# v_m summed in PSUM by one split-factor matmul per token and batch, and a softmax on VectorE and ScalarE alone

## The chip, the core and the metric

The kernel runs on one core of a Trainium2 chip. The metric is device time in microseconds, the median of several executions.

## What is computed

Attention over 32 memory slots per head, followed by a mixture-of-depths layer. Eight batches, 8 heads, 576 tokens, head dimension 64; the layer picks 128 tokens of each batch.

```python
a = phi - np.max(phi, axis=2, keepdims=True)          # over the tokens
a = np.exp(a)
a = a / (np.sum(a, axis=2, keepdims=True) + 1e-09)
k_m = np.einsum('bhsm,bhsd->bhmd', a, k)
v_m = np.einsum('bhsm,bhsd->bhmd', a, v)
scores = scale * np.matmul(q, k_m.transpose(0, 1, 3, 2))
attn = softmax(scores)                                # over the slots
x = np.matmul(attn, v_m)                              # then heads side by side: (B, S, 512)
# layer, per batch b:
scores[b] = x[b] @ w_gate
top_idx = np.argpartition(-scores[b], 128)[:128]
ye = np.maximum(x[b, top_idx] @ w1, 0.0) @ w2
out[b, top_idx] = x[b, top_idx] + sigmoid(scores[b, top_idx])[:, None] * ye
```

The choice of tokens hangs on the last bits of the scores, so the first softmax and v_m are computed in float32 with the reference's roundings.

## The kernel before

A group is four heads (two pairs) of a batch: 128 partitions of (head, slot) by 576 tokens. There are 16 groups, two to a batch.

`softmax(b, g)` (L161) computes a for a group. exp is a rational function whose multiply-adds are rounded once: `step_fma` (L192) splits both factors and carries the error, with ScalarE making the high halves, GpSimd nearly all products and differences (L198 to L209), VectorE one correction (L206). The quotient uses a reciprocal (L227) and more GpSimd work. At the end ScalarE and GpSimd make `half0` and `half1` (L261, L262), the high and low parts of a.

`keys(b, g)` (L268) transposes a to tokens on partitions (`aS`) and makes k_m, which goes into the block diagonal `kbd`.

`values(b, r, beside)` (L291) makes v_m of a pair of heads. For each of the 32 slots TensorE spreads the slot's row of a over 64 partitions for each head, by two float32r matmuls with the constant `sel` (L300), and VectorE multiplies that with v and sums over the tokens in one instruction (L303). After each slot `beside(m)` takes a step of the jobs that run between the sums: the next group's keys and softmax, and the attention and layer of the batch before.

`attention_and_ffn(b)` (L522) is `centre` (v_m less its mean, into `vbd`), three times `scores` and `attend`, then `rank`, `gather`, `ffn1`, `ffn2`. In `attend` GpSimd adds the means (L419); `score` (L386) makes the gate scores on VectorE (L389 to L394).

The order of instructions on each engine is the order of the program. Loads are issued on SyncE's queue; the stores of x and the indirect DMAs on GpSimd's. The weights w1 and w2 are loaded near the start by `late_consts`.

Of the kernel before, what the change touches and what calls it, by code (L numbers as in the profile page):

```python
# [13 lines left out]
I32 = mybir.dt.int32  # L14
AF = mybir.ActivationFunctionType
# [13 lines left out]
ROUND = 1.5 * 2.0 ** 23  # L29
# [4 lines left out]
EXP_LOWEST = -87.0  # L34


@with_exitstack
def kernel(
    ctx: ExitStack,
    tc: tile.TileContext,  # L40
    qT: bass.AP,      # [B, steps, (2h d), pairs, (2c p)], token p * NC + c
    k: bass.AP,       # [B, groups, p, c, (4h d)], token c * PT + p
    vT: bass.AP,      # [B, pairs, (2h d), s]
    phiT: bass.AP,    # [B, groups, (4h m), s]
# [3 lines left out]
    out: bass.AP,     # [B, S, D]  # L48
# [5 lines left out]
    PT = S // NC            # partitions of tokens  # L54
    NJ = qT.shape[1]        # steps of two columns of tokens
    NPR = vT.shape[1]       # pairs of heads
    NG = phiT.shape[1]      # groups of four heads, that is of two pairs
# [5 lines left out]
    HS = S // 2  # L63
# [3 lines left out]
    # The chosen tokens, in rows of at most 128 ranks.  # L67
# [5 lines left out]
    io = ctx.enter_context(tc.tile_pool(name="io", bufs=2))  # L73
    ex = ctx.enter_context(tc.tile_pool(name="ex", bufs=1))
    work = ctx.enter_context(tc.tile_pool(name="work", bufs=2))
    one = ctx.enter_context(tc.tile_pool(name="one", bufs=1))
    step = ctx.enter_context(tc.tile_pool(name="step", bufs=2))
    psb = ctx.enter_context(tc.tile_pool(name="psb", bufs=3, space=PSUM))
    pss = ctx.enter_context(tc.tile_pool(name="pss", bufs=2, space=PSUM))
# [4 lines left out]
    phis, ks, vs, qs = {}, {}, {}, {}  # L84

    def load_phi(b, g):
        phis[b, g] = io.tile([P, S], F32, name="ph")
        nc.sync.dma_start(out=phis[b, g], in_=phiT[b, g])

    def load_kv(b, g):  # L90
        ks[b, g] = io.tile([PT, NC, D // NG], F32, name="kb")
        nc.sync.dma_start(out=ks[b, g], in_=k[b, g])
        for r in (2 * g, 2 * g + 1):
            vs[b, r] = io.tile([P, S], F32, name="vb", bufs=4)
            nc.sync.dma_start(out=vs[b, r], in_=vT[b, r])

    def load_q(b, j):
        qs[b, j] = io.tile([P, NPR, 2 * PT], F32, name="qb", bufs=3)
        nc.sync.dma_start(out=qs[b, j], in_=qT[b, j])

    load_phi(0, 0)
    load_phi(0, 1)
    load_kv(0, 0)
    load_kv(0, 1)
# [5 lines left out]
    sel = const.tile([P, M, 2 * Dh], F32R, name="sel")  # L110
    nc.gpsimd.memset(sel.bitcast(F32), 0.0)
    for rr in range(2):
        for u in range(2):
            part = sel[:, :, u * Dh:(u + 1) * Dh]
            nc.gpsimd.affine_select(out=part, in_=part.bitcast(F32), compare_op=ALU.not_equal, fill=1.0,
                                    base=-(2 * rr + u) * M, pattern=[[-1, M], [0, Dh]],
                                    channel_multiplier=1)
    # k_m and v_m of several heads as block diagonals; what is off them stays zero.
    kbd = [const.tile([P, NPR, 2 * M], F32, name=f"kbd{i}") for i in range(2)]
    vbd = [const.tile([P, 2, NPR * Dh], F32, name=f"vbd{i}") for i in range(2)]  # L120
    for t in kbd + vbd:
        nc.vector.memset(t, 0.0)

    w1_sb = const.tile([P, KD, F], F32, name="w1_sb")
    w2_sb = const.tile([P, KF, D], F32, name="w2_sb")
# [5 lines left out]
    def late_consts():  # L131
# [3 lines left out]
        nc.sync.dma_start(out=w1_sb, in_=w1.rearrange("(t p) f -> p t f", p=P))  # L135
        nc.sync.dma_start(out=w2_sb, in_=w2.rearrange("(t p) f -> p t f", p=P))
# [4 lines left out]
        # wide[p, n] = 1 where n - (NC - 1) * PT < p.  # L141
# [9 lines left out]

    biases = {}
    for x in (EXP_P[0], EXP_P[1], EXP_P[2], EXP_P[4], EXP_Q[1], -1.0, -ROUND):
        biases[x] = constant(x)

    def fma(dst, src, s, c):
        nc.scalar.activation(dst, src, AF.Identity, bias=biases[c], scale=s)  # L157

    soft = {}

    def softmax(b, g):  # L161
        """a = exp(phi - max) / sum over the tokens, as numpy rounds it, and by pairs of heads
# [53 lines left out]
        for c in (EXP_P[2], EXP_P[1], EXP_P[0]):  # L216
            yield from step_fma(num, num, c)
# [387 lines left out]
```

## Time and profile before

| | |
|---|---|
| median of 3 runs | 1953.56 us (1953.15 to 1955.42) |
| span of the profiled execution | 1954.3 us |
| VectorE busy | 1352.5 us, 69% |
| GpSimd busy | 1041.0 us, 53% |
| TensorE busy | 996.6 us, 51% |
| ScalarE busy | 294.2 us, 15% |
| DMA | 52.0 MB, 27 GB/s on average |

The span runs from the first to the last instruction of one execution; the profiled execution's own time is known only by this span, which lies within the spread of the three runs. A busy share is a mean over stages whose limits differ. Matmuls are pipelined, so the busy time of TensorE counts overlapping records once and is not its throughput. [...]

### The profile page before, as it was taken

The numbers are of one execution on the slowest core, as the hardware profiler recorded it, in microseconds if no ns is written. First come the engines' busy times: TensorE is split into PE (matmuls) and PEld (weight loads), VectorE is DVE, ScalarE is ACT, GpSimd is POOL, SyncE is SP. The second block draws the span as 40 slices with busy tenths as digits, with TensorE's granted clock in tenths as the row PEclk, the third lists the DMA queues.
The fourth block names the chain that finished last, engine by engine and source line by source line (L and its number), as shares of the span: only waits on it lengthen the run. The fifth ranks groups of instructions, "written<-read, shape, count | busy, mean of one in ns | idle before, by whom it ended". The sixth has DMA issues, their size and how long they took to land. (4 is left out here: it accounts for less than half of the span.)

```text
span 1954.3 us, 13765 instructions
## 1 busy us (share of the span) xinstructions
PE 996.6 (51%) x4088; PEld 767.7 (39%) x4088; DVE 1352.5 (69%) x3052; ACT 294.2 (15%) x505; POOL 1041.0 (53%) x734
## 2 busy tenths in 40 slices
PE   0256363473635645366443655437463374634944
PEld 0244252352524434254432544325352352524733
DVE  2568677766876668757688567875687856877743
ACT  1111121111211112111120112101121111111010
POOL 8594837347473555627376092752927438373021
PEclk9955566575666657565665756657566575765666
DMA  4001011000000010010100101001010100100000
GB/s 152 12 7 37 11 33 30 24 24 30 27 17 24 24 32 26 16 36 12 43 22 8 42 6 43 22 9 42 6 43 22 32 24 18 44 18 6 6 16 19
DMA packets 17915, 52.00 MB, mean 27 GB/s; under 512 B 2096, under 2 KB 2096, under 8 KB 17840
## 3 DMA queue, kind: packets, MB, share of 16 engines
q1 hardware_dynamic: 13872, 37.49, 6.2%
q0 software_dynamic: 3968, 13.63, 2.3%
q8 instruction: 32, 0.52, 0.1%
q14 instruction: 43, 0.35, 0.1%
HBM read 39.58 MB, written 11.53 MB: 26 GB/s over the span
## 5 line engine op out<-in xcount | busy, mean ns | idle before, releaser
L300 PE MATMUL sp<-half,sel 128*128 128x288 f32 x2048 | 673.1, 473 | 706.5 <-DVE junk L303 546.7
L303 DVE SCALAR_TENSOR_TENSOR junk<-sp,vb 128x576 bf16<-128x576 f32 x1024 | 720.8, 748 | 233.5 <-PE sp L300 233.5
L300 PEld LDWEIGHTS sp<-half,sel 128*128 128x128 f32 x2048 | 469.8, 286 | 869.2 <-DVE junk L303 692.0
L389 DVE TENSOR_TENSOR prod<-xj,wg 96x1024 f32<-96x1024 f32 x24 | 113.7, 4736 | 101.8 <-POOL xj L419 101.8
L419 POOL TENSOR_TENSOR xj<-xj,mean 96x1024 f32<-96x1024 f32 x48 | 115.1, 2398 | 74.4 <-DVE xj L415 72.5
L190 POOL TENSOR_TENSOR rl<-r,rh 128x576 f32<-128x576 f32 x16 | 20.4, 1275 | 238.5 <-ACT rh L188 238.5
L208 POOL TENSOR_TENSOR low<-low,big 128x576 f32<-128x576 f32 x64 | 89.9, 1405 | 106.2 <-DVE big L206 102.9
L206 DVE SCALAR_TENSOR_TENSOR big<-s,big 128x576 f32<-128x576 f32 x64 | 67.9, 1061 | 110.3 <-ACT s L157 110.3
L262 POOL TENSOR_TENSOR half<-a,half 64x576 fp32r<-64x576 f32 x32 | 44.7, 1397 | 155.2 <-issue 141.6
L517 POOL DMA_INDIRECT out<-ye,idx x8 | 8.1, 1017 | 212.9 <-DVE ye L515 212.9
L204 POOL TENSOR_TENSOR low<-low,vl 128x576 f32<-128x576 f32 x64 | 109.3, 1708 | 5.0
L198 POOL TENSOR_TENSOR vl<-num,vh 128x576 f32<-128x576 f32 x48 | 61.2, 1276 | 86.5 <-ACT vh L197 86.5
L412 PE MATMUL bank<-vbd,eT 128*96 128x256 f32 x192 | 88.7, 616 | 31.4 <-ACT eT L406 31.4
L203 POOL TENSOR_TENSOR vl<-vl,r 128x576 f32<-128x576 f32 x64 | 104.4, 1632 | 0.0
L303 DVE DVE_READ_ACCUMULATOR junk<-sp,vb 128x1 f32 x1024 | 82.6, 81 | 0.0
L202 POOL TENSOR_TENSOR low<-vh,rl 128x576 f32<-128x576 f16 x64 | 82.4, 1287 | 0.2
L157 ACT ACTIVATE s<-big,c 128x576 f32<-128x576 f32 x64 | 49.5, 774 | 218.2 <-POOL big L199 218.2
L199 POOL TENSOR_TENSOR big<-vh,rh 128x576 f32<-128x576 f16 x64 | 81.3, 1271 | 0.0
L498 PE MATMUL bank<-xeT,w_sb 128*128 128x128 f32 x512 | 73.3, 313 | 13.7 <-ACT xeT L492 13.7
L498 PEld LDWEIGHTS bank<-xeT,w_sb 128*128 128x128 f32 x512 | 71.3, 227 | 15.8 <-ACT xeT L492 15.8
L209 POOL TENSOR_TENSOR num<-s,low 128x576 f32<-128x576 f32 x48 | 73.5, 1531 | 3.8
L434 PE MATMUL bank<-ident,gate 96*96 96x96 f32 x48 | 10.3, 307 | 123.2 <-DVE gate L394 113.4
(121 smaller groups left out, 1508.2 us busy)
## 6 DMA issues: line engine op xcount, KB each, us to landing
kb<-in_k SPq DMA_DIRECT2D x16, 576.0 KB, 4.5
vb<-in_vT SPq DMA_DIRECT2D x32, 288.0 KB, 2.8
qb<-in_qT SPq DMA_DIRECT2D x24, 384.0 KB, 4.4
out<-xj POOLq DMA_DIRECT2D x24, 384.0 KB, 3.3
ph<-in_phiT SPq DMA_DIRECT2D x16, 288.0 KB, 3.4
w_sb<-in_w SPq DMA_DIRECT2D x2, 2048.0 KB, 16.2
wg<-in_w_gate SPq DMA_DIRECT2D x1, 256.0 KB, 10.7
xe<-out,idx POOLq DMA_INDIRECT x8, 3.4
```

The lines of the kernel that those rows point to most:

```text
L199: nc.gpsimd.tensor_mul(big, vh, rh)
L202: nc.gpsimd.tensor_mul(low, vh, rl)
L203: nc.gpsimd.tensor_mul(vl, vl, r)
L204: nc.gpsimd.tensor_add(low, low, vl)
L208: nc.gpsimd.tensor_sub(low, low, big)
L209: nc.gpsimd.tensor_add(dst, s, low)
L300: nc.tensor.matmul(out=sp[:, hf, :HS], lhsT=sel[:, m], rhs=parts[:, hf * HS:(hf + 1) * HS], start=True, stop=True)
L303: nc.vector.scalar_tensor_tensor(out=junk, in0=sp[:, :, :HS], scalar=1.0, in1=vb.rearrange("p (a n) -> p a n", a=2), op0=ALU.mult, op1=ALU ...
L389: nc.vector.tensor_mul(prod[:n, :cols], rows, wg[:n].unsqueeze(1).to_broadcast([n, cols, D]))
L412: nc.tensor.matmul(out=o[:, u].rearrange("p r d -> p (r d)"), lhsT=eT[:, c, u], rhs=vbd[b % 2][:, u], start=True, stop=True)
L419: nc.gpsimd.tensor_add(x, x, t.unsqueeze(1).to_broadcast([PT, 2, D]))
L498: nc.tensor.matmul(out=ps[:, f, :n], lhsT=w1_sb[:, d, (f0 + f) * P:(f0 + f + 1) * P], rhs=xeT[:, d, :n], start=(d == 0), stop=(d == KD - 1))
```

## The change

- The reference's sum over tokens for v_m moves to TensorE. a and v are each split in a high and a low part (bits masked off, and the difference), so that a product of two parts is exact, and a matmul per token and batch, with the parts and heads on 32 rows, adds the four products of all 8 heads into a PSUM bank. The rows off the block diagonal of `a_rows` and half of `v_rows` stay zero.
- To have tokens in sequence and (head, part) on partitions, the parts go through DRAM: `split_v` writes `vparts` (each part twice), `keys` writes `aparts`, both from GpSimd's queue, and `values` reads them back in chunks of 36 tokens for four batches, from SyncE's queue, into two buffers.
- `sel`, the halves and VectorE's sums are gone. `centre` transposes v_m first.
- The softmax uses integer high parts on a grid (written as int16 by ScalarE), no GpSimd and no reciprocal of 576 columns.
- The order: `turns` interleaves two jobs, the second `lag` steps after the first; `beside` takes n steps of another job after each. Softmax of batches 0 to 3 with `split_v` of all batches; softmax of batches 4 to 7 with the sums of batches 0 to 3; attention of batches 0 to 3 with the sums of batches 4 to 7; attention of batches 4 to 7.
- GpSimd zeroes the tiles. w1 and w2 are loaded when the attention begins. `load_q` is issued by `scores`, a step ahead. `kbd` has a tile for each batch.

```diff
+    kbd = [const.tile([P, NPR, 2 * M], F32, name=f"kbd{i}") for i in range(B)]
+    v_rows = [rows.tile([P, 2, T, Dh], F32R, name=f"v_rows{i}") for i in range(2)]
+    a_rows = [rows.tile([P, T, NPR, M], F32R, name=f"a_rows{i}") for i in range(2)]
+    for t in v_rows + a_rows:
...
     def softmax(b, g):
+        r = phis.pop((b, g))
+        mx = ex.tile([P, 1], F32, name="mx")
+        nc.vector.tensor_reduce(mx, r, axis=AX.X, op=ALU.max)
+        nc.vector.tensor_scalar(out=r, in0=r, scalar1=mx, scalar2=EXP_LOWEST,
                                 op0=ALU.subtract, op1=ALU.max)
+        q = t("q", I16)
+        act(q, r, LOG2E)
+        yield
+        for ln2 in (LN2_HI, LN2_LO):
+            stt(out=r, in0=q, scalar=-ln2, in1=r, op0=ALU.mult, op1=ALU.add)
+        rh, rl = t("rh", I16), t("rl")
+        act(rh, r, 2.0 ** 11)
         num, den = t("num"), t("den")
+        act(num, r, EXP_P[5] * UP, EXP_P[4] * UP)
+        dh = t("dh", I16)
+        act(dh, r, EXP_Q[2] * UP * GRID, EXP_Q[1] * UP * GRID)
+        act(den, r, EXP_Q[2] * UP, EXP_Q[1] * UP)
+        yield
+        tt(out=num, in0=num, in1=r, op=ALU.mult)
+        vh = t("vh", I16)
+        act(vh, num, GRID, EXP_P[3] * UP * GRID)
+        act(num, num, 1.0, EXP_P[3] * UP)
+        stt(out=rl, in0=rh, scalar=-GRID, in1=r, op0=ALU.mult, op1=ALU.add)
+        def fma(val, h, c):
+            lo, big, low = t("lo"), t("big"), t("low")
+            stt(out=lo, in0=val, scalar=GRID, in1=h, op0=ALU.mult, op1=ALU.subtract)
+            tt(out=big, in0=h, in1=rh, op=ALU.mult)
+            tt(out=lo, in0=lo, in1=rh, op=ALU.mult)
+            tt(out=low, in0=val, in1=rl, op=ALU.mult)
+            tt(out=low, in0=low, in1=lo, op=ALU.add)
+            stt(out=val, in0=big, scalar=c * UP, in1=low, op0=ALU.add, op1=ALU.add)
+        yield
+        fma(den, dh, EXP_Q[0])
+        dh = t("dh", I16)
+        act(dh, den, GRID / 2)
+        y0 = t("y0", I16)
+        act(y0, r, 1.0, Y0_SCALE, AF.Exp)
         for c in (EXP_P[2], EXP_P[1], EXP_P[0]):
+            yield
+            fma(num, vh, c)
+            if c != EXP_P[0]:
+                vh = t("vh", I16)
+                act(vh, num, GRID)
+            if c == EXP_P[2]:
+                sq = t("rl2")
+                act(sq, den, 1.0 / UP, -1.5, AF.Square)
+        dl, p = t("lo"), t("big")
+        stt(out=dl, in0=den, scalar=GRID / 2, in1=dh, op0=ALU.mult, op1=ALU.subtract)
+        stt(out=p, in0=sq, scalar=0.75, in1=den, op0=ALU.add, op1=ALU.mult)
+        s2 = t("low")
+        act(s2, p, 1.0 / UP, -1.5, AF.Square)
+        tt(out=p, in0=y0, in1=dh, op=ALU.mult)
+        tt(out=num, in0=num, in1=p, op=ALU.subtract)
+        tt(out=dl, in0=y0, in1=dl, op=ALU.mult)
+        tt(out=num, in0=num, in1=dl, op=ALU.subtract)
+        two_q = t("den", I32)
+        yield
+        act(two_q, q, UP, 127 * UP)
+        stt(out=num, in0=s2, scalar=0.75, in1=num, op0=ALU.add, op1=ALU.mult)
+        stt(out=num, in0=sq, scalar=0.75, in1=num, op0=ALU.add, op1=ALU.mult)
+        stt(out=num, in0=num, scalar=GRID, in1=y0, op0=ALU.mult, op1=ALU.add)
+        sm = ex.tile([P, 4], F32, name="sm")
         e = t("e")
+        stt(out=e, in0=num, scalar=GRID / 2, in1=two_q.bitcast(F32),
+            op0=ALU.mult, op1=ALU.mult, accum_out=sm[:, 0:1])
...
         for i in (2, 3):
+            stt(out=e, in0=a0, scalar=sm[:, i:i + 1], in1=e, op0=ALU.mult, op1=ALU.add)
+        stt(out=e, in0=e, scalar=sm[:, 1:2], in1=a0, op0=ALU.mult, op1=ALU.add)
+        soft[b, g] = e
+        yield
+        yield from keys(b, g)
+    def split_v(b):
         for u in range(2):
+            vb = io.tile([P, S * Dh * NPR // P], F32, name="vb")
+            nc.sync.dma_start(out=vb, in_=v[b, u])
+            hi = io.tile([P, S * Dh * NPR // P], F32, name="vhi")
+            nc.vector.tensor_single_scalar(hi.bitcast(I32), vb.bitcast(I32), -4096,
+                                           op=ALU.bitwise_and)
+            nc.vector.tensor_sub(vb, vb, hi)
+            yield
+            for vp, src in enumerate((vb, hi)):
+                for ap in range(2):
+                    nc.gpsimd.dma_start(
+                        out=vparts[b, u, ap, vp].rearrange("r s d -> (r s d)")
+                                                .rearrange("(p x) -> p x", p=P), in_=src)
+            yield
...
     def keys(b, g):
...
+        hi = ex.tile([PT, NC, P], F32, name="ahi", bufs=1)
+        lo = ex.tile([PT, NC, P], F32, name="alo", bufs=1)
+        nc.vector.tensor_single_scalar(hi.bitcast(I32), aS.bitcast(I32), -4096,
+                                       op=ALU.bitwise_and)
+        nc.vector.tensor_sub(lo, aS, hi)
+        for h in range(4):
+            r, u = 2 * g + h // 2, h % 2
+            for part, src in enumerate((lo, hi)):
+                nc.gpsimd.dma_start(
+                    out=aparts[r, b, u, part].rearrange("(c p) m -> p c m", p=PT),
+                    in_=src[:, :, h * M:(h + 1) * M])
...
+    def values(st):
+        accs = [accp.tile([P, 512], F32, name=f"acc{i}") for i in range(SET)]
+        b0 = st * SET
+        def load(ch):
+            ss = slice(ch * T, (ch + 1) * T)
+            for vp in range(2):
+                for r in range(NPR):
+                    nc.sync.dma_start(
+                        out=a_rows[ch % 2][vp * 4 + r::8, :, r].bitcast(F32),
+                        in_=aparts[r, b0:b0 + SET].rearrange("b u t s m -> (b u t) s m")[:, ss])
+            for bb in range(SET):
+                for u in range(2):
+                    p0 = bb * 32 + u * 16
+                    nc.sync.dma_start(
+                        out=v_rows[ch % 2][p0:p0 + 16, u].rearrange("p s d -> p (s d)").bitcast(F32),
+                        in_=vparts[b0 + bb, u].rearrange("t w r s d -> (t w r) (s d)")
+                            [:, ch * T * Dh:(ch + 1) * T * Dh])
+        n = S // T
+        load(0)
+        for ch in range(n):
+            if ch + 1 < n:
+                load(ch + 1)
+            vr, ar = v_rows[ch % 2], a_rows[ch % 2]
+            for s in range(T):
+                for bb in range(SET):
+                    p = slice(bb * 32, bb * 32 + 32)
+                    nc.tensor.matmul(out=accs[bb][:, :P].rearrange("p (u d) -> p u d", d=Dh),
+                                     lhsT=ar[p, s].rearrange("p r m -> p (r m)"), rhs=vr[p, :, s],
+                                     start=(ch == 0 and s == 0), stop=(ch == n - 1 and s == T - 1))
+                if s % 4 == 3:
+                    yield
+        for bb in range(SET):
+            v_m[b0 + bb] = const.tile([P, P], F32, name=f"v_m{b0 + bb}")
+            nc.scalar.activation(v_m[b0 + bb], accs[bb][:, :P], AF.Copy)
...
+        tp = bank([P, P])
+        nc.tensor.transpose(out=tp, in_=v_m.pop(b), identity=ident)
+        vm = work.tile([P, NPR, M], F32, name="vmT")
+        nc.scalar.activation(vm.rearrange("p r m -> p (r m)"), tp, AF.Copy)
...
+    def turns(jobs, lag, width=2):
+        jobs, live, since = list(jobs), [], lag
+        while jobs or live:
+            if jobs and len(live) < width and since >= lag:
+                live.append(jobs.pop(0))
+                since = 0
+            since += 1
+            for job in list(live):
+                if next(job, live) is live:
+                    live.remove(job)
+                else:
+                    yield
+    def beside(main, other, n):
+        for _ in main:
+            for _ in range(n):
+                next(other, None)
+            yield
+    def group(i):
+        if i + 2 < len(groups):
+            load_phi(*groups[i + 2])
+        load_k(*groups[i])
+        yield from softmax(*groups[i])
...
+    half = len(groups) // 2
+    finish(beside(turns([group(i) for i in range(half)], 6),
+                  chain(*[split_v(b) for b in range(B)]), 1))
+    sums = values(0)
+    finish(beside(turns([group(i) for i in range(half, 2 * half)], 6), sums, 2))
+    finish(sums)
+    first.close()
+    w1_sb = one.tile([P, KD, F], F32, name="w1_sb")
+    w2_sb = one.tile([P, KF, D], F32, name="w2_sb")
+    nc.sync.dma_start(out=w1_sb, in_=w1.rearrange("(t p) f -> p t f", p=P))
+    nc.sync.dma_start(out=w2_sb, in_=w2.rearrange("(t p) f -> p t f", p=P))
+    def batch(b):
+        load_q(b, 0)
+        yield from attention_and_ffn(b)
+    sums = values(1)
+    finish(beside(turns([batch(b) for b in range(SET)], 10), sums, 2))
+    finish(sums)
+    finish(turns([batch(b) for b in range(SET, B)], 10))
...
```

`act(dst, src, s, c, func)` is a ScalarE activation of s * src + c; `tt` and `stt` are VectorE's tensor_tensor and scalar_tensor_tensor. SET is 4, T is 36.

## Rows read from the trace of the kernel before

**Rows 1.** The page: span, and its first part (busy share of each engine).

```profile
span 1954.3 us, 13765 instructions
...
PE 996.6 (51%) x4088; PEld 767.7 (39%) x4088; DVE 1352.5 (69%) x3052; ACT 294.2 (15%) x505; POOL 1041.0 (53%) x734
```

**Rows 2.** Window of one batch: stretch, length, PE, PEld, DVE, ACT, POOL busy, clock, DMA.

```profile
301.00:523.00 222.00, 119.41 (x500) 92.21 (x498) 159.12 (x365) 34.35 (x59) 119.54 (x84) 0.62 0.08 24
```

**Rows 3.** Waits in that batch: who waited for whom, us in total, times, longest.

```profile
DVE junk L303 <- PE sp L300: 31.9, 16, 7.3
...
ACT s L157 <- POOL big L199: 26.7, 7, 7.9
...
PE sp L300 <- POOL half L262: 10.2, 2, 5.2
...
DVE prod L389 <- POOL xj L419: 10.2, 2, 5.1
```

**Rows 4.** Groups by form: busy us, mean ns of one, idle before.

```profile
L303 DVE SCALAR_TENSOR_TENSOR junk<-sp,vb 128x576 bf16<-128x576 f32 x1024 | 720.8, 748 | 233.5 <-PE sp L300 233.5
...
L206 DVE SCALAR_TENSOR_TENSOR big<-s,big 128x576 f32<-128x576 f32 x64 | 67.9, 1061 | 110.3 <-ACT s L157 110.3
...
L227 DVE RECIPROCAL s<-den 128x576 f32<-128x576 f32 x16 | 59.8, 3740 | 0.0
...
L178 DVE SCALAR_TENSOR_TENSOR x<-q,x 128x576 f32<-128x576 f32 x16 | 12.0, 752 | 7.2 <-ACT q L157 7.2
...
L174 DVE TENSOR_SCALAR q<-x 128x576 f32<-128x576 f32 x16 | 9.2, 572 | 0.5
```

**Rows 5.** Window of the last batch's attention and layer.

```profile
1859.00:1954.30 95.30, 41.51 (x195) 31.77 (x195) 36.94 (x81) 9.96 (x21) 17.64 (x11) 0.64 0.06 18
```

**Rows 6.** Timeline at the start: start us, length us, engine, line.

```profile
1.34 3.50 POOL L111 MEMSET sel<- 128x4096 f32 x1
...
1.73 0.42 SPq L92 DMA_DIRECT2D kb<-in_k  x1
```

**Rows 7.** Windows of the weight loads (w1, then w2).

```profile
14.00:18.00 4.00, 0.00 (x0) 0.00 (x0) 1.89 (x3) 1.95 (x3) 1.01 (x1) 1.00 1.03 409
...
18.00:24.00 6.00, 0.00 (x0) 0.00 (x0) 0.46 (x1) 1.24 (x2) 4.71 (x5) 1.00 1.04 390
```

**Rows 8.** DMA queues and issues, and the issuing group on GpSimd.

```profile
q1 hardware_dynamic: 13872, 37.49, 6.2%
...
out<-xj POOLq DMA_DIRECT2D x24, 384.0 KB, 3.3
...
L422 POOL DMA_DIRECT2D out<-xj x24 | 13.6, 565 | 0.9 <-POOL xj L419 0.9
```

**Rows 9.** TensorE's rate: windows of L498 alone, timelines of L511, L364 and L300.

```profile
1932.20:1935.20 3.00, 3.00 (x14) 3.00 (x15) 0.50 0.02 5
...
1937.60:1940.60 3.00, 3.00 (x30) 3.00 (x29) 1.00 0.00 0
...
1940.91 7.03 PE L511 MATMUL bank<-w_sb,hT 128*128 128x512 f32 x16
...
1865.06 5.27 PE L364 MATMUL bank<-kbd,qb 128*96 128x64 f32 x32
...
1008.13 1.52 PE L300 MATMUL sp<-half,sel 128*128 128x288 f32 x4
```

**Rows 10.** Sources L300 and L498, weight loads: shortest/median/longest ns.

```profile
L300 PEld LDWEIGHTS sp<-half,sel x2048: 185/289/368, 79.5 to 1857.3; 128*128 128x128 f32 x187
...
L498 PEld LDWEIGHTS bank<-xeT,w_sb x512: 186/192/339, 388.3 to 1940.7; 128*128 128x128 f32 x171
```

**Rows 11.** Window of L300 alone, the last sums.

```profile
1839.00:1857.00 18.00, 18.00 (x55) 13.35 (x54) 0.50 0.00 0
```

**Rows 12.** Timelines of L389, in the body (GpSimd computing) and in the last batch.

```profile
314.31 6.67 DVE L389 TENSOR_TENSOR prod<-xj,wg 96x1024 f32<-96x1024 f32 x1 [5.08 <-POOL xj L419]
...
1884.88 1.22 DVE L389 TENSOR_TENSOR prod<-xj,wg 96x1024 f32<-96x1024 f32 x1 [4.94 <-POOL xj L419]
```

More of the change, by code (lines that the diff above doesn't have):

```diff
@@ L72 @@
     const = ctx.enter_context(tc.tile_pool(name="const", bufs=1))
[L73 to L79, printed above, removed]
+    rows = ctx.enter_context(tc.tile_pool(name="rows", bufs=1))
@@ L88, in load_phi, with load_k @@
         nc.sync.dma_start(out=phis[b, g], in_=phiT[b, g])
[L90 removed]
+    def load_k(b, g):
         ks[b, g] = io.tile([PT, NC, D // NG], F32, name="kb")
         nc.sync.dma_start(out=ks[b, g], in_=k[b, g])
[L93 to L95 removed]
     def load_q(b, j):
[L98 removed]
+        qs[b, j] = step.tile([P, NPR, 2 * PT], F32, name="qb", bufs=4)
@@ L99, in load_q @@
         nc.sync.dma_start(out=qs[b, j], in_=qT[b, j])
[L101 to L104, printed above, removed]
+    groups = [(b, g) for b in range(B) for g in range(NG)]
+    for bg in groups[:2]:
+        load_phi(*bg)
     ident = const.tile([P, P], F32, name="ident")
     make_identity(nc, ident)
[L110 to L117, printed above, removed]
@@ L224, in softmax @@
-        fma(dh, den, 1.0, -1.0)
-        nc.vector.scalar_tensor_tensor(out=dl, in0=den, scalar=1.0, in1=dh,
-                                       op0=ALU.subtract, op1=ALU.subtract)
-        nc.vector.reciprocal(rec, den)
-        prod, rem = t("big"), t("low")
-        nc.gpsimd.tensor_sub(num, num, y0)
-        nc.gpsimd.tensor_mul(prod, y0, dh)
-        nc.gpsimd.tensor_sub(rem, num, prod)
-        nc.gpsimd.tensor_mul(dl, y0, dl)
-        nc.gpsimd.tensor_sub(rem, rem, dl)
-        nc.gpsimd.tensor_mul(rem, rem, rec)
@@ L284, in keys @@
                                  start=(c == 0), stop=(c == NC - 1))
[L285 removed]
+        yield
         for u in range(2):
[L287 to L307 removed]
+            part = slice(u * Dh, (u + 1) * Dh)
+            nc.scalar.activation(kbd[b][part, 2 * g:2 * g + 2, u * M:(u + 1) * M],
+                                 km[part, :, u * M:(u + 1) * M], AF.Copy)
@@ L539, in finish @@
             pass
-    finish(softmax(0, 0))
-    late_consts()
-    behind = iter(())
-    for b in range(B):
-        for g in range(NG):
-            last = g == NG - 1
-            if last and b + 1 < B:
-                load_phi(b + 1, 0)
-                load_phi(b + 1, 1)
-            ahead = [keys(b, g)]
-            if b + last < B:
-                ahead.append(softmax(b + last, (g + 1) % NG))
-            ahead = chain(*ahead)
-            def beside(m):
-                if m % 3 == 0:
-                    next(ahead, None)
-                if m % 2:
-                    next(behind, None)
-            for r in (2 * g, 2 * g + 1):
-                values(b, r, beside)
-            finish(ahead)
-            if b + 1 < B:
-                load_kv(b + 1, g)
-        finish(behind)
-        for j in range(NJ):
-            load_q(b, j)
-        behind = attention_and_ffn(b)
@@ new lines, in finish @@
+    def finish(job):
+        for _ in job:
+            pass
+    def group(i):
[3 more added lines that the diff above has]
+        yield from softmax(*groups[i])
+    late_consts()
+    half = len(groups) // 2
[4 more added lines that the diff above has]
+    finish(sums)
@@ new lines @@
+    first.close()
+    work = ctx.enter_context(tc.tile_pool(name="work", bufs=2))
+    one = ctx.enter_context(tc.tile_pool(name="one", bufs=1))
+    step = ctx.enter_context(tc.tile_pool(name="step", bufs=2))
+    w1_sb = one.tile([P, KD, F], F32, name="w1_sb")
[5 more added lines that the diff above has]
+        yield from attention_and_ffn(b)
```

147 lines of the change are left out of this document (37 added, 110 removed).

## The prediction

> **What bounds the kernel now.** I read the page's busy line first, then one batch by a window, then who waited for whom inside one batch, then the costs by form. No engine is full: VectorE is busy 69% of the span, TensorE 51%, GpSimd 53% [rows 1]. The body is one pattern repeated, a batch each 222 us; in one of them VectorE is busy 159 us, GpSimd 119.5 and TensorE 119.4 [rows 2]. So what is to be seen is a busiest engine that still idles 63 us a batch. Inside the batch VectorE's longest waits are for TensorE's product (31.9 us) and for GpSimd's addition of the means (10.2 us); TensorE in turn stands behind the halves that GpSimd makes at the end of a softmax (10.2 us), and ScalarE waits 26.7 us for GpSimd's products in the middle of it [rows 3]. VectorE's largest single item is L303: 1024 sums of 748 ns, 721 us (803 with the accumulator reads) [rows 4]. The bound is thus VectorE's sums plus a softmax whose chain runs through GpSimd. The last batch's attention and layer stand alone at the end, 95.3 us [rows 5].
>
> **How the changed kernel is laid out.** It is no longer one pattern. In order: A, groups 0 to 7 of the softmax, with the splitting of v beside it; B, groups 8 to 15, with the sums of batches 0 to 3 beside it; C, attention of batches 0 to 3, with the sums of batches 4 to 7 beside it; D, attention of batches 4 to 7 alone. Two jobs are interleaved in each. I cost the four in turn.
>
> **VectorE in a softmax group.** Removed: the 3.74 us reciprocal, the 4 slow L206, and GpSimd's whole share. Counting the new code, a group has 41 two-input operations of 576 columns: 2 for ln 2, 1 product, 1 for rl, 4 x 6 in the fma's, 10 in the division and the product with 2^q, 3 for the quotient. L178 costs one at 752 ns; L206, the same operation at 1061 ns, is the bound from above, since it runs while GpSimd computes, which GpSimd no longer does here. 41 x 0.753 = 30.9. The maximum, the subtraction, five operations of one column, and the two that split aS (768 columns) add 0.75 + 0.53 + 0.8 + 1.8. Sum 34.8 us a group (47 at L206's price), against some 17 us now: the work of GpSimd moves onto VectorE. I take 34.8.
>
> **A.** 8 x 34.8 = 278. The split of v is 16 pieces of 1152 columns, 1.15 + 1.5 us each by twice L174 and L178 [rows 4]: 42. At the start GpSimd zeroes four tiles of 4608 columns, by L111 [rows 6] 3.9 us each, before the biases that ScalarE needs: 16. Drain of the last job, where no second one covers ScalarE: 14. A = 350. What lies beside it: 64 writes of v parts, 37.7 MB, and 9.4 MB of v read; at the 390 to 409 GB/s of the weight loads [rows 7] 118 us, which must fit beside the 32 steps among which split_v is dealt out (about 110 us), so A's upper end is 400. GpSimd issues 8 DMAs a group of 576 pieces of 128 B; by L422 (0.57 us for 96 pieces) [rows 8] between 0.57 us each if the piece count does not matter and 3.4 us if it does, 5 to 27 us a group, hidden under 34.8 either way.
>
> **The chunk, c.** The sums run in chunks of 36 tokens and four batches, 16 chunks in B and 16 in C, double-buffered, so the pace is the slower of matmuls and loads. *Matmuls:* 144 pairs of a weight load (128 columns) and a product (128 columns), float32r, on 32 rows each. The nearest row is L511: 16 float32 products of 512 columns in 7.03 us at the full clock, 0.86 ns a column, 110 ns for 128; at the half clock L498 starts 14 in 3.00 us, 214 ns [rows 9]. A float32r column is cheaper (L300: four products of 288 columns in 1.52 us at half clock, at most 1.32 ns a column), but L364 shows weights setting the pace: 32 products of only 64 columns take 165 ns each at half clock [rows 9], and float32r weights load as long as float32 ones, shortest 185 against 186 ns [rows 10]. So I take the float32 price. Bounds: a quarter of 110 (28 ns), if the four row groups fully overlap, and 214 at the half clock. The clock: L498's run of 64 is at 0.50 at 1932 us and at 1.00 by 1937.6 [rows 9], and the runs here are longer; L300, with gaps after each pair, stays at 0.50 [rows 11]. I take 120 ns, full clock nearly throughout: c = 17.3 us. *Loads:* 1.18 MB of v in rows of 9 KB, 3 us by rows 7; 0.59 MB of a in 4608 pieces of 128 B, 288 per DMA engine. The trace has no such piece. By bytes alone 5 ns each, 1.5 us in all; by the mean packet of the SP queue (6.2% of 16 x 1954.3 us over 13872 packets) [rows 8] 140 ns, 40 us. Rows 7 show pieces of 4 KB and of 2 KB at nearly one rate (409 and 390 GB/s), so the fixed cost of a piece is small; I take the geometric middle, 27 ns, 7.8 us. Sixteen issues of 0.42 us [rows 6] make 6.8 us, beside it. Loads 11 us: under the matmuls.
>
> **B.** First chunk late by 40 us: group 7's last DMAs (up to 27), their landing 3.3 [rows 8], the load. TensorE then has 16c plus 24 us of transposes and k_m; two steps of sums per softmax step use up the 144 steps after 72, that is after 6.5 of the 8 groups, and 1.5 groups of VectorE follow (52). The keys' transposes stand behind the sums in TensorE's queue, and VectorE's split of aS behind them, so the two engines proceed together. B = 116 + 16c (floor: VectorE's 278 + some 35).
>
> **C and D.** One batch alone has VectorE busy 36.9 us, TensorE 41.5, in 95.3 [rows 5]. Two at a time lie between 41.5 and 95.3 a batch; I take 62.5, for the queues are in order, and VectorE's product takes 6.67 us instead of 1.22 where GpSimd computes [rows 12]; here GpSimd still has the additions. D = 250. C's sums are dealt out over the first 72 of some 148 steps: 16c, 80 for the TensorE work of two batches in the same queue, 20 for the weights (4 MB), now loaded here ahead of the first chunk, then 125 for batches 2 and 3. C = 225 + 16c.
>
> **Sum.** A 350 + B 116 + C 225 + D 250 = 941, and 32c. With c = 17.3: **1495 us**, against the span of 1954.3; the median of the runs, 1953.56, is within 1 us of that span, so nothing is added around it.
>
> **The rivals.** *Row groups overlap.* Each of the four batches uses other rows and another bank. If they run side by side, the loads set c = 11: 941 + 352 = 1293, about 1300. For: the code alternates the groups. Against: no row shows matmuls on part of the rows. [...]
> *The half clock stays.* Every wait for a chunk is a gap, and rows 11 show 18 us of busy TensorE at 0.50. Then c = 30.7, 941 + 982 = 1923: almost all the gain gone.
> *Slower: small pieces.* One mechanism: a 128-byte piece of the a-rows holds its DMA engine so long that the loads set c. The point of decision is 32c = 1013, c = 31.7, so (31.7 - 3) / 288 = 100 ns a piece. At the mean packet's 140 ns c = 43 and the time is 941 + 1376 = 2317. For: 140 is what packets here take on average. Against: those packets carry 2.7 KB, and rows 7 show time following bytes. [...]
> *The change does not free VectorE.* If its operations cost L206's 1061 ns, 16 groups cost 202 us more, half of them hidden under B's sums: about 1600, inside the forecast's neighbourhood.
>
> **How the numbers follow.** Forecast (c 15 to 20, 1400 to 1620 with A's and D's bounds) 0.43; row groups overlap 0.27; half clock 0.13; small pieces 0.13; the rest, between these, 0.04. The range goes from 1200 (overlap, with D at 45 us a batch and A without stalls) to 1930 (half clock); left out are the small pieces and tails beyond the low end, under 2 in 10. About 0.2% (4 us; the runs shown spread over 2.3) is what a measurement can tell from no change. Faster: 0.43 + 0.27 + most of 0.13 and 0.04, 0.86; same 0.01; slower 0.13.
>
> **What would show it.** In the changed profile: two-input VectorE operations of the softmax near 0.75 us and VectorE over 85% busy in A; float32r pairs 110 to 120 ns apart with the granted clock near 1.0 in B and C (below 60 overlap, at 214 half clock); TensorE waiting on earlier work rather than on the a-rows' DMAs; small DMA packets well under 100 ns; a last stretch of 250 us without sums. The prediction is wrong if TensorE's waits in B and C are for a_rows, or if A is far above 400 because the writes of the parts hold it.

## The result, and the profile after

The changed kernel takes 1416.77 us (median of 4 runs, 1415.52 to 1419.14) against 1954.49 for the kernel before in the same session (1953.15 to 1955.80): a ratio of 0.7252, 95% interval 0.7241 to 0.7262, 538 us less. The forecast was 1495 us, the range 1200 to 1930.

The page of the changed kernel: span, busy shares, the clock's and the DMA's row of the 40 slices, and q1 (SyncE's DMA queue: packets, MB, share of 16 engines), to lay beside [rows 1, 8]; the last two lines are shares of the chain of work that ended last.

```profile
span 1415.6 us, 16937 instructions
...
PE 724.6 (51%) x6656; PEld 617.9 (44%) x6656; DVE 874.7 (62%) x1480; ACT 272.4 (19%) x489; POOL 297.8 (21%) x312
...
PEclk9999999999999999999999999978757755678567
DMA  6798811112999898930788888781110111010100
...
DMA packets 190718, 156.05 MB, mean 110 GB/s; under 512 B 160560, under 2 KB 162608, under 8 KB 186544
...
q1 hardware_dynamic: 171312, 94.15, 37.1%
...
DVE 34%; PE 24%; DMA 14%; SPq 12%; POOL 8%; issue 4%; ACT 3%; DVEq 0%; POOLq 0%; ACTq 0%
DMA v_rows<-vparts 9%; SPq L314 8%; PE acc L334 8%; POOL xj L458 7%; PE bank L537 5%; PE bank L550 3%; SPq L320 3%; PE bank L451 2%; PE bank L294 2%; DVE low L194 2%; DVE lo L190 2%; DVE low L193 2%; PE bank L503 2%; DVE big L191 2%; DVE lo L192 2%
```

VectorE falls from 1352.5 to 874.7 us, GpSimd from 1041.0 to 297.8, TensorE from 996.6 to 724.6. What is new is the DMA row: 9 and 8 tenths in the slices where the sums run, and in the chain the rows of v (9%) and SyncE's issue of the a-rows (8%).

Windows of it by stage, as the prediction cuts it: A up to the first sum, the sums in B, the rest of B's softmax, then (after 24.4 us to C's first sum) the sums in C, the rest of C, and D. Columns as in [rows 2, 5].

```profile
4.60:366.30 361.70, 54.93 (x240) 49.98 (x241) 321.32 (x457) 99.74 (x161) 99.47 (x154) 1.00 0.51 170
366.30:622.70 256.40, 184.41 (x2480) 172.29 (x2484) 204.23 (x319) 73.22 (x117) 34.77 (x48) 1.00 0.95 143
622.70:682.00 59.30, 14.34 (x73) 12.85 (x69) 47.58 (x84) 16.27 (x31) 11.60 (x16) 1.00 0.11 19
706.40:964.00 257.60, 216.32 (x2619) 184.58 (x2620) 75.79 (x156) 20.17 (x45) 35.95 (x21) 0.95 0.80 132
964.00:1120.00 156.00, 92.82 (x471) 71.85 (x469) 73.45 (x146) 21.59 (x48) 37.33 (x22) 0.74 0.12 38
1120.00:1415.60 295.60, 161.79 (x783) 126.27 (x783) 150.98 (x317) 40.12 (x87) 74.76 (x45) 0.69 0.11 35
```

In B the DMA engines are busy 95% of the time and TensorE 72%: the loads set the pace of the sums, 256.4 us for 16 chunks, 16.0 each. C's sums take 257.6, no longer, although two attention jobs run beside them. The granted clock, as a share of TensorE's full one, is 1.00 throughout A and B, 0.95 in C's sums, and 0.74 and 0.69 in what follows them.

VectorE by form, to lay beside [rows 4]: an addition in the softmax's multiply-adds, and its product of int16 parts.

```profile
L194 DVE TENSOR_TENSOR low<-low,lo 128x576 f32<-128x576 f32 x64 | 48.5, 758 | 2.2
...
L191 DVE TENSOR_TENSOR big<-vh,rh 128x576 f32<-128x576 int16 x48 | 36.0, 750 | 0.0
```

Both take 750 to 758 ns; the 1061 of L206 in the kernel before, beside GpSimd, does not come back.

Timeline of TensorE in B: four first products of a chunk, one for each batch, and a run of full speed.

```profile
443.21 0.44 PE L334 MATMUL acc<-v_rows,a_rows 32*128 32x128 f32 x1 [3.42 <-issue]
445.32 0.44 PE L334 MATMUL acc<-v_rows,a_rows 32*128 32x128 f32 x1 [1.66 <-DMA v_rows<-vparts]
447.45 0.44 PE L334 MATMUL acc<-v_rows,a_rows 32*128 32x128 f32 x1 [1.69 <-DMA v_rows<-vparts]
449.55 1.11 PE L334 MATMUL acc<-v_rows,a_rows 32*128 32x128 f32 x13 [1.65 <-DMA v_rows<-vparts]
...
460.95 11.36 PE L334 MATMUL acc<-v_rows,a_rows 32*128 32x128 f32 x208
```

In the run, 208 pairs of weight load and product take 11.36 us; the last product is 0.41 of it, so they start (11.36 - 0.41) / 207 = 53 ns apart. Before it the first product of a chunk waits for each batch's rows of v in turn, 2.1 us apart. The waits of TensorE in B say the same (us in total, times, longest), as do the DMA issues (times, KB, us to landing):

```profile
PE acc L334 <- DMA v_rows<-vparts: 78.1, 43, 13.6
```

```profile
v_rows<-vparts SPq DMA_DIRECT2D x256, 144.0 KB, 6.0
...
a_rows<-aparts SPq DMA_DIRECT2D x256, 72.0 KB, 3.8
```

### The profile page after: what moved, and what is told of

It is laid out like the page before. It is cut to its first block, busy times and chain, and to the rows that moved or that the text cites. A ratio compares the mean times of both kernels' runs of the same rounds, so it can differ in the third digit from the quotient of the medians.

```text
span 1415.6 us, 16937 instructions
## 1 busy us (share of the span) xinstructions
PE 724.6 (51%) x6656; PEld 617.9 (44%) x6656; DVE 874.7 (62%) x1480; ACT 272.4 (19%) x489; POOL 297.8 (21%) x312
## 3 DMA queue, kind: packets, MB, share of 16 engines
q1 hardware_dynamic: 171312, 94.15, 37.1%
## 4 chain that ended last, share of the span: by engine, by line
DVE 34%; PE 24%; DMA 14%; SPq 12%; POOL 8%; issue 4%; ACT 3%; DVEq 0%; POOLq 0%; ACTq 0%
DMA v_rows<-vparts 9%; SPq L314 8%; PE acc L334 8%; POOL xj L458 7%; PE bank L537 5%; PE bank L550 3%; SPq L320 3%; PE bank L451 2%; PE bank L294 2%; DVE low L194 2%; DVE lo L190 2%; DVE low L193 2%; PE bank L503 2%; DVE big L191 2%; DVE lo L192 2%
## 5 line engine op out<-in xcount | busy, mean ns | idle before, releaser
L334 PE MATMUL acc<-v_rows,a_rows 32*128 32x128 f32 x4608 | 286.5, 409 | 143.0 <-DMA v_rows<-vparts 132.6
L334 PEld LDWEIGHTS acc<-v_rows,a_rows 32*128 32x128 f32 x4608 | 264.6, 319 | 172.9 <-issue 136.3
L458 POOL TENSOR_TENSOR xj<-xj,mean 96x1024 f32<-96x1024 f32 x48 | 118.7, 2476 | 308.7 <-DVE xj L454 229.4
L288 POOL DMA_DIRECT2D aparts<-alo x64 | 47.1, 736 | 444.1 <-DVE alo L284 444.1
L294 PE MATMUL bank<-aS,kb 96*128 96x64 f32 x384 | 86.1, 423 | 11.7 <-ACT aS L278 11.7
L294 PEld LDWEIGHTS bank<-aS,kb 96*128 96x128 f32 x384 | 83.1, 331 | 16.5 <-ACT aS L278 15.8
L428 DVE TENSOR_TENSOR prod<-xj,wg 96x1024 f32<-96x1024 f32 x24 | 37.8, 1576 | 68.0 <-POOL xj L458 68.0
L537 PE MATMUL bank<-xeT,w_sb 128*128 128x128 f32 x512 | 73.1, 314 | 7.0 <-ACT xeT L531 7.0
L537 PEld LDWEIGHTS bank<-xeT,w_sb 128*128 128x128 f32 x512 | 71.4, 229 | 10.1 <-ACT xeT L531 10.0
L403 PE MATMUL bank<-kbd,qb 128*96 128x64 f32 x384 | 57.2, 332 | 8.9 <-DMA qb<-in_qT 8.9
L403 PEld LDWEIGHTS bank<-kbd,qb 128*96 128x96 f32 x384 | 56.1, 247 | 10.7 <-issue 9.1
L550 PE MATMUL bank<-w_sb,hT 128*128 128x512 f32 x128 | 56.5, 594 | 0.0
L194 DVE TENSOR_TENSOR low<-low,lo 128x576 f32<-128x576 f32 x64 | 48.5, 758 | 2.2
```

Of the source, the lines that this page charges most:

```text
L194: tt(out=low, in0=low, in1=lo, op=ALU.add)
L288: nc.gpsimd.dma_start(out=aparts[r, b, u, part].rearrange("(c p) m -> p c m", p=PT), in_=src[:, :, h * M:(h + 1) * M])
L294: nc.tensor.matmul(out=km[:, rr], lhsT=kb[:, c, rr * P:(rr + 1) * P], rhs=aS[:, c, rr * 2 * M:(rr + 1) * 2 * M], start=(c == 0), stop=(c = ...
L334: nc.tensor.matmul(out=accs[bb][:, :P].rearrange("p (u d) -> p u d", d=Dh), lhsT=ar[p, s].rearrange("p r m -> p (r m)"), rhs=vr[p, :, s], ...
L403: nc.tensor.matmul(out=sc[:, c, :, r], lhsT=qb[:, r, c * PT:(c + 1) * PT], rhs=kbd[b][:, r], start=True, stop=True)
L458: nc.gpsimd.tensor_add(x, x, t.unsqueeze(1).to_broadcast([PT, 2, D]))
```

## The experiments

Theory after this reading: four row groups of TensorE (32 rows each) work side by side, so a pair of weight load and product costs 53 to 55 ns, and the loads set c, the time of a chunk; the rows of v are the slow part of them, because a DMA of v writes 16 neighbouring partitions. Rivals: the small pieces of a set the pace and v stands behind them; 55 ns is simply what a float32r pair costs; the order of the jobs, and not the loads, is what costs the time.

**1. What a pair costs.** All matmuls read rows 0 to 31:

```diff
-                    p = slice(bb * 32, bb * 32 + 32)
+                    p = slice(0, 32)
```

> All matmuls of the sums read rows 0 to 31, so batches 1 to 3 get the values of batch 0 (v_m is wrong for them); the number of matmuls, their columns, the loads and the order stay. Theory (a pair costs 55 ns only because four row groups work at once): now a pair takes 213 ns, as where only one batch's v had landed, 144 pairs 30.7 us a chunk; B = 40 + 16 x 30.7 + 24 + part of the softmax tail, C likewise, so 1800 to 1900 in all. Rival (55 ns is what one float32r pair of 128 columns costs at the full clock, whatever rows it uses): 1417, no change.

2001.62 us, 102% of the kernel before (1955.15 beside it) and more than the 1800 to 1900 expected. TensorE's timeline in B, and a window of B:

```profile
521.79 8.52 PE L334 MATMUL acc<-v_rows,a_rows 32*128 32x128 f32 x39
```
```profile
500.00:890.00 390.00, 390.00 (x1813) 386.24 (x1813) 148.48 (x229) 52.83 (x86) 29.05 (x40) 1.00 0.40 67
```

39 pairs take 8.52 us, (8.52 - 0.41) / 38 = 213 ns apart, at a granted clock of 1.00 and with TensorE busy without a pause. It is four times the 53 of the kernel as changed. So on the same 32 rows a float32r pair costs 213 ns, and the gain of the whole change hangs on four of them running at once. Why 213 is twice the 100 ns at which L498's float32 pairs start at the full clock (30 in 3.00 us in [rows 9]) no run here shows.

Does the order in which batches alternate matter? Four tokens of one batch in a row, then four of the next:

```diff
-            for s in range(T):
-                for bb in range(SET):
+            for s0 in range(0, T, 4):
+                for bb, s in [(bb, s0 + i) for bb in range(SET) for i in range(4)]:
```

> Nothing left out: four tokens of one batch follow each other, then four of the next, so that four matmuls in a row use the same 32 rows. Theory (the four row groups run side by side: 55 ns a pair in the changed kernel, 208 in 11.4 us): pairs now 105 to 112 ns apart in a run, as float32 products of 128 columns at the full clock; a chunk's matmuls 15.5 instead of 8 us, under or near the loads' 16 but behind them in a chain of two buffers, so time 1440 to 1560. Rival (55 ns is simply the price of one float32r pass of 128 columns at the full clock): pairs stay at 55 ns and the time at 1410 to 1425.

1421.21 us, and in the timeline:

```profile
442.52 1.08 PE L334 MATMUL acc<-v_rows,a_rows 32*128 32x128 f32 x4 [3.91 <-issue]
...
460.73 11.55 PE L334 MATMUL acc<-v_rows,a_rows 32*128 32x128 f32 x208
```

The expectation was wrong: with all rows landed, 208 pairs take 11.55 us, 54 ns apart, as before. But at 442.52, when only one batch's rows of v had landed, four pairs take 1.08 us: (1.08 - 0.41) / 3 = 0.22 us apart, the price of experiment 1. So with four row groups a pair costs the same whether the group changes at each instruction or at every fourth, 53 and 54 ns: the order of these did not matter, and this run alone told nothing apart.

**2. What the loads cost.** Without v, and without a, after the first two chunks of each half (the products then use stale rows; 28 of 32 chunks load nothing, where the second expectation says 30):

```diff
-            for bb in range(SET):
+            for bb in range(SET if ch < 2 else 0):
```

> Left out: the loads of v_rows after the first two chunks of each half (v_m is wrong). Theory (the v packets are the largest share of a chunk's DMA time, 7.4 of 16 us, the 128-byte pieces 4.75 to 5.2): the loads come down to about 8 us a chunk, B to VectorE's pace (some 14.5 us a chunk), C's sums to what two batches of attention take (150 us instead of 258); time 1280 to 1320. Rival (the 128-byte pieces set the pace): 16 us a chunk stays at 14 or more in C, time over 1380.

```diff
-            for vp in range(2):
+            for vp in range(2 if ch < 2 else 0):
```

> The a-rows are loaded for the first two chunks only; the later chunks multiply stale a-rows (v_m is then wrong), everything else stays. It takes away 30 of 32 chunks' 128-byte pieces, 129,024 packets. Theory (the pieces are cheap, some 13 ns each; the rows of v, about 1 us for 9216 bytes, make most of a chunk's load): the queue's share of the DMA engines falls by 30 x 288 x 13 ns to 17 ns = 112 to 147 us of 1416, 8 to 10 points from 37; a chunk falls from 16 us to about 11, and the kernel to 1340 to 1375, no more than without the loads of v (1349). Rival (the small pieces set the pace, so that v only waits behind them): the sums fall as far as VectorE and TensorE let them, and v's packets shorten too; below 1335.

1349.46 us without v and 1351.65 without a. The line of q1 without v, then without a:

```profile
q1 hardware_dynamic: 164144, 61.10, 21.5%
```

```profile
q1 hardware_dynamic: 38704, 77.62, 29.0%
```

A share times its span is the time per DMA engine: 525.2 us in the changed kernel (37.1% of 1415.6), 289.8 without v, 391.5 without a. So 3584 rows of v cost 235.4 x 16, 1051 ns for each 9216 bytes (their own packets last 925 ns on average; most of the rest is that a's pieces take 14.3 ns instead of 16.5 when v is gone); 129,024 pieces of a cost 133.7 x 16, 16.6 ns each. A chunk's 128 rows of v and 4608 pieces are 8.4 and 4.8 us per engine; with the stores of a's parts, phi and k, which run then too, this fills the 16.0. Small pieces are cheap, but either load gone brings the time down by 65 to 67 us, and no further: without v the sums of B still take 224 us (366.0 to 590.0) and those of C 214 (679.6 to 893.9), and in the last 204 of these TensorE is busy 196:

```profile
690.00:894.00 204.00, 195.95 (x2532) 168.85 (x2528) 75.79 (x156) 19.10 (x40) 35.97 (x21) 0.97 0.39 78
```

The next bound stands close behind: in B VectorE, whose groups follow each other every 35.8 us without v, in C TensorE's two jobs. That is also why the time stayed above the 1280 to 1320 expected without v.

**3. Why a row of v is slow.** The same bytes, the same number of DMAs, but the 16 partitions of a DMA are 8 apart (v's rows are then misplaced among the batches):

```diff
-                        out=v_rows[ch % 2][p0:p0 + 16, u].rearrange("p s d -> p (s d)").bitcast(F32),
+                        out=v_rows[ch % 2][2 * bb + u::8, u].rearrange("p s d -> p (s d)").bitcast(F32),
```

> Left out: nothing is left out, but the rows of v are put into other partitions (every eighth instead of sixteen neighbours), so v_m is not the reference's. In the changed kernel the v_rows packets of 9216 bytes take about 925 ns each in 400 to 600 us and the loads set a pace of 16 us a chunk. [...] Rival 1 (SyncE's 16 issues, 12 us a chunk, set the pace) and rival 2 (the DRAM side of these rows is slow): packets stay near 925 ns or the pace near 16 us, and the time at 1410 to 1425.

1369.66 us, 47 less. The same lines, first of this run, then of one with the rows in another order, in which nothing is misplaced:

```profile
q1 hardware_dynamic: 171312, 94.15, 29.4%
...
v_rows<-vparts SPq DMA_DIRECT2D x256, 144.0 KB, 3.5
```

```diff
+            for u in range(2):
+                nc.sync.dma_start(
+                    out=v_rows[ch % 2][u::2, u].rearrange("p s d -> p (s d)").bitcast(F32),
+                    in_=vparts[u, b0:b0 + SET].rearrange("b t w r s d -> (b t w r) (s d)")
+                        [:, ch * T * Dh:(ch + 1) * T * Dh])
```

> Same sums, but the part index u is made the lowest bit of the row, so that one DMA of v writes 64 partitions, every second of 128, instead of 16 neighbours; two DMAs a chunk instead of eight, and a's parts are written to DRAM twice (16 DMAs a group on GpSimd instead of 8). [...] Rival (the larger number of issues and writes on GpSimd's queue costs what the loads save): 1370 to 1420.

```profile
q1 hardware_dynamic: 168240, 94.13, 26.5%
...
v_rows<-vparts SPq DMA_DIRECT2D x64, 576.0 KB, 5.1
```

1366.57 us, between the 1335 to 1365 expected and the rival's 1370 to 1420. Packets of 9216 bytes in the three traces:

```
partitions of one DMA of v         median ns   mean ns
16 neighbours (changed kernel)        1012       925
16, 8 apart                            564       557
64, 2 apart                            347       443
```

The first step, from 16 neighbours to 16 that lie 8 apart, changes nothing but the partitions and takes 44% off the median and 40% off the mean. The second takes off another 38% and 20%, but it also makes two DMAs a chunk out of eight. Why neighbouring partitions are slower no run here shows. C's sums, 257.6 us in the changed kernel, take 232 in the first of these runs and 219 in the second. The last kernel gains 50 us although its a-parts are written twice to DRAM and its first sum starts later, at 379.7 instead of 366.3; and since the run before it issues as many DMAs as the changed kernel, the fewer issues on SyncE are not what gains.

**4. The order in C and D.** One step of the sums for each step of attention, in place of two:

```diff
-    finish(beside(turns([batch(b) for b in range(SET)], 10), sums, 2))
+    finish(beside(turns([batch(b) for b in range(SET)], 10), sums, 1))
```

> Nothing left out: in C one step of the sums, not two, follows each step of attention, so that the sums of batches 4 to 7 last over all four batches (144 of some 148 steps). Theory (C is 258 us of load-bound sums with two batches beside them, then 160 us of two batches with nothing beside them, while the DMA engines idle): C becomes 290 to 330 us instead of 438, time 1290 to 1330. Rival (attention waits for the sums in TensorE's queue, so stretching the sums stretches it too): C 400 or more, time 1390 to 1430.

1370.45 us. Windows of C and D:

```profile
679.00:1072.00 393.00, 313.83 (x3090) 251.63 (x3088) 152.88 (x316) 43.18 (x95) 76.24 (x48) 0.81 0.60 118
1072.00:1368.00 296.00, 163.52 (x783) 128.44 (x783) 151.21 (x317) 40.22 (x87) 74.86 (x45) 0.69 0.12 35
```

C falls from 440.6 to 393.0 us, less than half of what was expected, and the time lies between theory and rival; D stays at 296. The sums now end at 1050, 22 us before the end of C, where they ended 156 before it: more of the attention runs beside them and less is left to run alone.

The offset between two attention jobs, 18 steps in place of 10, in C and D:

> The second attention job starts 18 steps after the first instead of 10, in C and in D. Theory (the two jobs of D run in step, so that both want the same engine in turn and both wait for GpSimd at the same time; 293 us for four batches instead of the predicted 250): D changes by 10 us or more, down if the collision is at fault, up if what counts is only that the last job runs alone longer (8 steps of 74 more, some 10 us). Rival (D is a sum of dependent chains and the offset does not matter): within 5 us of 1417.

1408.74 us, 8 less, of which D gains 4 (1115.7 to 1407.0 by the start of its first operation, L352, instead of 1120.1 to 1415.6). The theory wanted 10 us or more in D, the rival within 5 us of 1417 in all; neither holds as it stands, but two jobs that run in step explain at most these 4 us of D.

**5. Each half of the change alone.** The kernel before with only the softmax exchanged, and the changed kernel with only the old softmax put back:

```diff
+        a = work.tile([P, S], F32, name="a")
+        stt(out=a, in0=e, scalar=sm[:, 1:2], in1=a0, op0=ALU.mult, op1=ALU.add)
+        halves = []
```

> One half of the change alone: the kernel before, with its sums on VectorE, and only the softmax (up to a and the two halves) replaced by the new one. Theory (before, VectorE waits for GpSimd's chain, so work moved onto it partly fills idle time): VectorE's busy time is 1352.5 + 16 x (33 - 17) = 1608 us, and with the waits for TensorE's products, 32 us a batch, the kernel takes 1700 to 1870, faster than 1954. Rival (VectorE is the bound, and what moves onto it adds up): 1954 + 256 = 2210.

```diff
+        soft[b, g] = a
+        yield
+        yield from keys(b, g)
...
-    finish(beside(turns([group(i) for i in range(half, 2 * half)], 6), sums, 2))
+    finish(beside(turns([group(i) for i in range(half, 2 * half)], 6), sums, 1))
```

> The other half alone: the changed kernel, with its sums in PSUM, and only the softmax (up to a) replaced by the old one with its GpSimd products; in B one step of the sums per step of the longer job instead of two. Theory (GpSimd needs some 51 us a group, 101.9 us of a batch's 119.5 less the attention's 17.6, so it sets the pace in A and B): A 430 to 450 instead of 366, B 440 to 470 instead of 315; 1590 to 1650 in all. Rival (GpSimd's products run beside VectorE's work and the DMA sets B): 1417 within 20.

1887.62 us with the new softmax and the old sums, 1873.59 with the old softmax and the new sums (1955.25 for the kernel before beside them). Both were expected to be faster, 1700 to 1870 and 1590 to 1650, and neither rival (2210, 1417) came either. The page of the first, and windows of two groups of the second, in A and in B:

```profile
span 1885.9 us, 13345 instructions
...
PE 1039.3 (55%) x4088; PEld 795.6 (42%) x4088; DVE 1508.0 (80%) x3468; ACT 293.8 (16%) x505; POOL 205.8 (11%) x143
...
L304 DVE SCALAR_TENSOR_TENSOR junk<-sp,vb 128x576 bf16<-128x576 f32 x1024 | 719.8, 750 | 196.2 <-PE sp L301 195.6
```

```profile
199.70:330.10 130.40, 13.64 (x60) 12.49 (x60) 48.99 (x51) 23.64 (x38) 118.10 (x91) 1.00 0.09 23
723.90:854.50 130.60, 51.68 (x700) 48.77 (x700) 48.89 (x51) 23.76 (x38) 118.24 (x91) 1.00 0.55 84
```

With the old sums VectorE is busy 80% and still waits 196 us for TensorE's products: a batch takes 231.5 us (from the sum at the end of one softmax's exp, L242, at 412.1 to the one five batches later at 1569.6) instead of 235.5 (L239, 366.1 to 1543.8), and the first sum for v_m starts at 50.9 instead of 80.4. VectorE's busy time rises by 156 us, not by the 256 expected: its gate product, 24 times L389, takes 4.74 us on average in the kernel before, where GpSimd's softmax runs beside it, and 1.22 here (L390), 84 us less in all.

With the old softmax a group takes 65 us whether sums run beside it or not, GpSimd busy 91% of them: 59 us a group, not the 51 that I took from [rows 2, 5]. That window of 222 us is shorter than the batch's 235.5; over the whole span it is (1041.0 / 8 - 17.6) / 2 = 56, less 2.8 for the halves, and 5.9 for eight issues of a-parts at 0.74 come on top.

So the halves alone are worth 68 and 82 us and both together 538. In the first, VectorE's sums still set the pace of a batch. In the second, GpSimd's softmax sets that of A and B: C begins at 1132.8 instead of 679.4, nearly the whole 457 us that this run loses against the changed kernel. But GpSimd needs only 130 us for the two groups of a batch, against the 235.5 of a batch in the kernel before; it costs so much here because the new order runs no attention beside the softmax. What the new sums would be worth with the old softmax in the old order, no run shows.

**6. Together.** The new order of the rows with one step in C; then also a piece of v loaded a step before it is split, its steps spread out, and the offset of 18:

> The layout of the run before (rows ordered so that a DMA of v writes every second of 128 partitions), and in C one step of the sums per step of attention instead of two. Theory (in C the first batches' attention goes slowly while the sums run two steps at a time, and what is left of it then runs alone; one at a time spreads it: 46 us less with the slow loads): C, 410 us in the run before, falls to 370 to 390; 1320 to 1347 in all. Rival (with quick loads nothing is left to gain, the sums being no longer late): 1360 to 1370.

```diff
             nc.sync.dma_start(out=vb, in_=v[b, u])
+            yield
...
+            if u:
+                yield
...
-    finish(beside(turns([batch(b) for b in range(SET)], 10), sums, 1))
+    finish(beside(turns([batch(b) for b in range(SET)], 18), sums, 1))
...
-    finish(turns([batch(b) for b in range(SET, B)], 10))
+    finish(turns([batch(b) for b in range(SET, B)], 18))
```

> The kernel with the new rows and one step in C, and two more edits: split_v loads a piece of v one step before it splits it and takes three to four steps a piece instead of two; the second attention job starts 18 steps after the first. Theory: VectorE's 21.6 us of waits for the pieces of v in A vanish, and a later start is worth 4 to 8 us as it was by itself; 15 to 30 us below the kernel without the two edits. Rival (the stalls of A are the DMA engines' own time for the parts, which merely moves): within 8 us of it.

1346.87 us with the first two, at the upper end of what was expected (C takes 393.5 us, above the 370 to 390), and 1310.94 with the further edits (4 runs, 1309.01 to 1311.33; ratio to the kernel before 0.6702, interval 0.6691 to 0.6714). Windows of A, B, C and D of the last:

```profile
4.50:363.60 359.10, 54.95 (x244) 49.98 (x244) 325.46 (x463) 101.20 (x163) 145.90 (x218) 1.00 0.61 186
363.60:638.80 275.20, 177.51 (x2526) 170.50 (x2526) 243.75 (x384) 86.69 (x143) 81.10 (x112) 1.00 0.65 147
638.80:1017.30 378.50, 301.07 (x3109) 245.70 (x3108) 151.80 (x318) 43.40 (x95) 85.10 (x59) 0.76 0.46 124
1017.30:1309.40 292.10, 157.06 (x783) 123.50 (x783) 152.63 (x317) 40.21 (x87) 75.50 (x45) 0.68 0.12 36
```

Beside quick loads one step in C is worth 20 us (1366.57 to 1346.87), not the 46 it gave beside slow ones: the two gains overlap. The further edits give 36 us, above the 15 to 30 expected: 17 in A (the first sum at 363.6 instead of 381.0), 15 in C (378.5 for 393.5), 4 in D (292.1 for 296.4).

## Why the prediction came out as it did

The measured 1417 us lie in the forecast's own band, 1400 to 1620, but by luck: the loads set the chunk, not the matmuls, and the errors of the terms cancel. The sum by its own terms, in us, against the windows above:

| term | predicted | measured |
|---|---|---|
| A and the wait for the first chunk | 350 + 40 | 366.3 |
| sums in B | 16 x 17.3 + 24 | 256.4 |
| softmax after them | 52 | 59.3 |
| C until its first sum | 20 | 24.4 |
| sums in C | 16 x 17.3 + 80 | 257.6 |
| rest of C | 125 | 156.0 |
| D | 250 | 295.6 |
| sum | 1495 | 1415.6 |

**The softmax: right.** 41 operations at 0.75 us; a group every 35.8 us once the split of v is over (34.8 forecast). While the parts of v are written it is 50, and the ninth group starts at 349.4, where A's forecast put it (350); the first chunk is late by 17, not 40. VectorE is busy 321.3 of A's 361.7 us.

**The pair: the step that failed.** I took the float32 price, 120 ns, from full-height products, and let the loads hide beneath. No run shows that price for a pair on 32 rows: in one row group pairs start 213 ns apart, in four row groups 53. The rival of overlapping row groups, to which I gave 0.27, is what happens; experiment 1 shows it, and shows also that without it the change would have lost 46 us. The matmuls of a chunk take 144 x 53 ns = 7.6 us.

**The loads: sized too small, and by the wrong half.** For v I took bytes at the best rate seen, 3 us a chunk; it is 8.4 (experiment 2), since a row takes 1012 ns in the median where its DMA writes 16 neighbouring partitions, and 564 where they lie 8 apart (experiment 3). For a I took 27 ns a piece, 7.8 us; it is 16.6 ns, 4.8 us. The sum of 11 is near 13.2, the stores beside it fill the rest. So c = 16.0 stands near the 17.3 forecast by chance: the loads set it, not the matmuls. Of the signs that the prediction names, TensorE's waits for DMAs came, but for v's rows (78.1 us in B, 54.5 in C's sums) and not for a's. The rival's own sum, 941 + 32 x 16.0 = 1453, is 36 above the result.

**C: its addition was wrong.** I added 80 us of TensorE's attention work to the sums. With the loads as the bound it lies beside them, and C's sums take what B's do; with 19 us from c this makes the 99. B's 44 are the same: 20 from c, and 24 of transposes and k_m that the loads cover.

**The rest of C and D: 31 and 46 us too small.** D takes 73.9 us a batch, inside the bounds of 41.5 and 95.3. The offset of the jobs explains 4 us of it; VectorE is busy 151.0 us of it and TensorE 161.8, so neither is full. In the chain of work that ends last, GpSimd's additions of the means (L458) make 20% of D, more than any other line, TensorE's products of the layer (L537, L550) 16% and VectorE's gate scores (L428, L430) 9%: engines that work in turn. No run shortens one of these, so what would bring D down stays open. Dealing the sums out one step at a time instead of two is worth 48 us in C (experiment 4).

The errors were -24, -44, +7, +4, -99, +31 and +46: they cancel to -79. The other rivals: the granted clock was 1.00 in B's sums and 0.95 in C's, the small pieces cost 16.6 ns where 100 would have decided, and VectorE's operations cost 0.75 us without GpSimd beside them.

## What to carry to other kernels

Where a change takes work off two engines, price its halves together and in the order in which they will run: here each alone gave under 85 us and both gave 538. A matmul on a quarter of the rows was cheap here only with three others beside it (53 ns a pair, 213 on the same rows), so look for the row groups before taking a price from full-height products. When data goes through DRAM and back, price a row by the partitions that one DMA writes, not by its bytes, and let them lie spread over all 128: the same 9216 bytes took 1012 ns here with 16 neighbours, 564 with 16 that lay 8 apart and 347 with 64 that lay 2 apart (medians).

## What the runs showed of the hardware

A float32r weight load and product of 128 columns on 32 rows took 213 ns a pair at the full clock when all pairs used the same rows (experiment 1), and 53 ns with four row groups; whether the program changed the group at each instruction or at every fourth made no difference (53 and 54 ns). Pieces of 128 bytes took 16.6 ns each on q1 (experiment 2), 9216 bytes in the median 1012 ns where a DMA wrote 16 neighbouring partitions, 564 with 16 that lay 8 apart and 347 with 64 that lay 2 apart (experiment 3). VectorE's product of 96x1024 took 4.74 us on average beside GpSimd's softmax and 1.22 without it (experiment 5).
